# The first product of the second mixture as seven half-size products, its outputs whole in six banks

## The chip, the cores and the metric

One core of a Trainium2 chip runs the whole program. The metric is the device time of one execution in microseconds (us). "Measured" means the median of repeated executions; the profile is of a single execution, taken by the hardware profiler.

## The reference

Three parts follow each other. Attention with 32 packed queries gives `x` (2304 tokens of 512). A first mixture of four experts and a second one then follow, in float32:

```python
p = domain_probs / (domain_probs.sum(-1) + 1e-9)
for e in range(4):                                   # first mixture, w1[e] 512x1024, w2[e] 1024x512
    out += p[:, e:e+1] * (np.maximum(x @ w1[e], 0) @ w2[e])
h = out @ w_in                                       # second mixture, w_in 512x2048 (float64 in DRAM)
g = h - np.tanh(h)
result = g @ w_out                                   # w_out 2048x512 (float64 in DRAM)
```

## The kernel before, in words

Every product keeps float32 accuracy on TensorE by splitting both operands in a high and a low part: three matmuls (high by high, high by low, low by high) stand for one. TensorE's order of instructions is written out by hand, up to the end of the first mixture, as strings of letters (`START_A` to `LAST`), each of which calls one function. The other engines are ordered by a scheduler.

**First mixture** (to 690 us). Half of a half of the experts' features is worked on at a time, in two passes over the tokens. Its up products (`up_prod`, L469) are already made as seven half-size products (Strassen and Winograd's scheme), in matmuls of 288 columns; its down products (`down`, L527, matmul at L535) have 512 columns. Beside it `decode` (L331), called through `background` at each "_" of the strings, reads w_in and w_out as 64-bit words, rebuilds float32 from them with DVE, ACT and POOL, splits them, and stores high and low part in DRAM.

**Second mixture** (from 690 us). The 2304 tokens are 18 tiles of 128, taken in units of 4, 4, 4, 4 and 2; the 2048 features are halved (`cc`). An item is a unit, a half and two blocks of 128 features: 40 items. `s3` (L724) makes h of an item: per block 12 matmuls of 512 columns (the tokens; 256 in the last unit), K in four pieces of 128, three parts each. That is 640 + 320 matmuls at L734, 768 of them of 512 columns and 192 of 256. `elem` (L743) reads h straight from PSUM and makes g = h − tanh(h) of it (a polynomial where h is small, L751 to L760, up to 1024 wide); `elem_split` (L763) splits g in `gh` (ACT) and `gl` (DVE); `s4` (L777) multiplies by w_out into one PSUM tile per token tile, 864 matmuls of 512 columns at L790. The partial outputs of cc = 0 go through ACT (L803) to DRAM and are added on DVE (L807) at cc = 1. A half's weights lie in 16 SBUF tiles, loaded once. `x_T` (L557) transposes and splits a unit's tokens.

```python
for n in range(N + 2):
    s3(items[n]); x_T(...)        # TensorE: h of item n
    elem_split(items[n - 1]); elem(items[n])
    s4(items[n - 2])              # TensorE: outputs of the item before the last
```

PSUM has eight banks of [128, 512] float32; a tile [128, 2, 512] takes two of them.

## Time and profile before

| what | value |
|---|---|
| measured, median of 3 | 1092.18 us (1091.44 to 1094.64) |
| the profiled execution's own time | 1094.34 us |
| its span | 1092.6 us |
| TensorE's mean granted clock | 0.995 of full speed |
| first matmuls of the second mixture | 690.4 us |
| DMA in the whole program | 113.5 MB |

In the profile, a "group" is all instructions of one line, engine and tile; "<-" names the tile that an engine waited for, and who filled it. PE is TensorE, DVE the vector engine, ACT the scalar engine, POOL GpSimd, SP the engine that issues DMAs.

### The profile page before, as it was taken

How to read it: one execution, taken by the hardware profiler on the slowest of the kernel's cores; microseconds unless marked ns; L12 is line 12 of the kernel's file. 1: busy time of each engine (PE TensorE's matmuls, PEld its weight loads, DVE VectorE, ACT ScalarE, POOL GpSimd, SP SyncE). 2: the span in 40 equal slices, each digit the busy share in tenths (PEclk: the TensorE clock that was granted, in tenths of full speed). 3: DMA queues.
4: the chain of work that ended last, by engine and by line, in shares of the span. 5: the costliest groups of instructions: out<-in, count | busy, mean ns of one | idle time of the engine just before them, and what ended most of it. 6: DMA issues, size and time to landing. Idle time of an engine off the chain costs nothing.

```text
span 1092.6 us, 15816 instructions
## 1 busy us (share of the span) xinstructions
PE 1080.0 (99%) x6308; PEld 894.8 (82%) x6308; DVE 809.5 (74%) x1134; ACT 573.6 (53%) x853; POOL 215.3 (20%) x137
## 2 busy tenths in 40 slices
PE   8899999999999999999999999999999999999998
PEld 6677888888888878888888888888888888888887
DVE  4567888787787775888888786587676767777775
ACT  3345454544555355445545553466657556656464
POOL 0101223432542232334344332000000000000000
PEclk9899999999999999999999999999999999999999
DMA  9434124324333223332423321601001262202102
GB/s 342 174 93 174 59 78 145 128 75 154 125 107 135 78 77 97 116 136 84 151 94 121 130 96 64 283 1 39 5 35 39 78 231 97 77 1 77 64 14 77
DMA packets 38281, 113.51 MB, mean 104 GB/s; under 512 B 4288, under 2 KB 4288, under 8 KB 38208
## 3 DMA queue, kind: packets, MB, share of 16 engines
q1 hardware_dynamic: 38208, 112.51, 29.2%
q8 instruction: 49, 0.80, 0.3%
q14 instruction: 24, 0.20, 0.1%
HBM read 86.28 MB, written 26.21 MB: 103 GB/s over the span
## 4 chain that ended last, share of the span: by engine, by line
PE 85%; ACT 1%; DMA 0%; DVE 0%; issue 0%; DVEq 0%; SPq 0%
PE yps L535 32%; PE h3ps L734 18%; PE ops L790 18%; PE hpx L485 7%; PE hpz L485 6%; PE wps L390 2%; PE hps L437 1%; PE xps L570 1%; DMA wraw<-in_w_dram 0%; ACT wph L413 0%; PE qtp L314 0%; DVE p L496 0%; ACT w2h L143 0%; DVEq L873 0%; DVE f L350 0%
## 5 line engine op out<-in xcount | busy, mean ns | idle before, releaser
L734 PE MATMUL h3ps<-xh,ws 128*128 128x512 f32 (+1 forms) x640 | 186.7, 368 | 0.0
L790 PE MATMUL ops<-ws,gh 128*128 128x512 f32 x576 | 174.9, 391 | 0.0
L734 PEld LDWEIGHTS h3ps<-xh,ws 128*128 128x128 f32 x640 | 116.5, 188 | 20.2
L144 POOL TENSOR_TENSOR w2l<-wraw,w2h 128x1024 fp32r<-128x1024 f32 x32 | 82.4, 2576 | 246.2 <-ACT w2h L143 246.2
L546 DVE SCALAR_TENSOR_TENSOR x<-yps,pn,x 128x512 f32<-128x512 f32 x126 | 93.9, 745 | 43.3 <-PE yps L535 42.5
L790 PEld LDWEIGHTS ops<-ws,gh 128*128 128x128 f32 x576 | 107.2, 188 | 21.9 <-ACT gh L769 0.2
L535 PE MATMUL yps<-w2h,h0h 128*128 128x512 f32 x288 | 117.5, 408 | 1.9 <-DVE a2l L318 1.4
L734 PE MATMUL h3ps<-xl,ws 128*128 128x512 f32 (+1 forms) x320 | 117.7, 368 | 0.0
L535 PE MATMUL yps<-w2h,h0l 128*128 128x512 f32 x288 | 113.2, 393 | 0.0
L535 PE MATMUL yps<-w2l,h0h 128*128 128x512 f32 x288 | 112.8, 392 | 0.0
L535 PE MATMUL yps<-w2h,h1h 128*128 128x512 f32 x288 | 112.8, 391 | 0.0
L535 PE MATMUL yps<-w2h,h1l 128*128 128x512 f32 x288 | 112.4, 390 | 0.0
L535 PE MATMUL yps<-w2l,h1h 128*128 128x512 f32 x288 | 112.1, 389 | 0.0
L790 PE MATMUL ops<-ws,gl 128*128 128x512 f32 x288 | 108.7, 389 | 0.0
L769 ACT ACTIVATE gh<-g 128x512 fp32r<-128x512 f32 (+1 forms) x80 | 45.6, 583 | 84.3 <-DVE g L760 84.3
L535 PEld LDWEIGHTS yps<-w2h,h0h 128*128 128x128 f32 x288 | 54.1, 188 | 33.7 <-issue 21.0
L362 POOL TENSOR_TENSOR fo<-fo 128x512 f32<-128x512 f32 x32 | 43.3, 1352 | 193.6 <-DVE fo L358 105.7
L756 DVE SCALAR_TENSOR_TENSOR g<-z,h3ps 128x1024 f32<-128x1024 f32 (+1 forms) x40 | 44.5, 1113 | 43.0 <-ACT t L752 42.8
L770 DVE TENSOR_TENSOR gl<-g,gh 128x512 fp32r<-128x512 f32 (+1 forms) x80 | 49.8, 634 | 34.3 <-ACT gh L769 34.2
L751 ACT ACTIVATE z<-h3ps 128x1024 f32<-128x1024 f32 (+1 forms) x40 | 37.6, 941 | 68.5 <-PE h3ps L734 64.8
L734 PEld LDWEIGHTS h3ps<-xl,ws 128*128 128x128 f32 x320 | 60.3, 188 | 10.3
L535 PEld LDWEIGHTS yps<-w2h,h0l 128*128 128x128 f32 x288 | 54.0, 188 | 12.1
(156 smaller groups left out, 2402.0 us busy)
## 6 DMA issues: line engine op xcount, KB each, us to landing
wraw<-in_w_dram SPq DMA_DIRECT2D x64, 512.0 KB, 4.6
f<-in_win_dram SPq DMA_DIRECT2D x16, 512.0 KB, 4.6
win<-fo SPq DMA_DIRECT2D x16, 512.0 KB, 2.9
f<-in_wout_dram SPq DMA_DIRECT2D x16, 512.0 KB, 4.6
wout<-fo SPq DMA_DIRECT2D x16, 512.0 KB, 2.9
ws<-win SPq DMA_DIRECT2D x16, 512.0 KB, 5.3
ws<-wout SPq DMA_DIRECT2D x16, 512.0 KB, 5.3
kt<-in_kT_dram SPq DMA_DIRECT2D x16, 288.0 KB, 5.9
```

The source lines that it names most:

```text
L144: (eng or nc.vector).tensor_tensor(out=lo, in0=src, in1=f(hi), op=ALU.subtract)
L362: nc.gpsimd.tensor_tensor(out=lf, in0=lf, in1=sq, op=ALU.mult)
L390: nc.tensor.matmul(out=ps[32 * j:32 * j + 32, r, :], lhsT=ppbd[p][d, bi, j, 32 * r:32 * r + 32], rhs=raw[0, c, j // 2][d, j % 2, :],)
L485: nc.tensor.matmul(out=ps[:, ff, 0:HB], lhsT=W[a][:, slot, c0], rhs=x[b], start=(start and k == 0), stop=(stop and k == 2), skip_group_che ...
L535: nc.tensor.matmul(out=ps, lhsT=a[:, ff, o:o + 128], rhs=w[c, fp][:, ff], start=(k == 0), stop=(k == 11),)
L546: last[0] = nc.vector.scalar_tensor_tensor(out=x2[tt], in0=ps, scalar=pn[:, tt, e:e + 1], in1=x2[tt], op0=ALU.mult, op1=ALU.add,).ins
L734: nc.tensor.matmul(out=ps[:, ff, 0:n], lhsT=w[:, wl, kd, :], rhs=x[:, kd, :], start=(k == 0), stop=(k == 11),)
L751: nc.scalar.activation(out=z, in_=h, func=ACTF.Square)
L756: nc.vector.scalar_tensor_tensor(out=g, in0=z, scalar=C4, in1=h, op0=ALU.mult, op1=ALU.mult)
L769: nc.scalar.activation(out=hs[ff][:, 0:n], in_=g[:, ff], func=ACTF.Copy)
L770: nc.vector.tensor_tensor(out=ls[ff][:, 0:n], in0=g[:, ff], in1=f(hs[ff][:, 0:n]), op=ALU.subtract)
L790: nc.tensor.matmul(out=ops[u][t], lhsT=a[ff][:, d], rhs=w[:, wl], start=(i == 0 and ff == 0 and k == 0), stop=(i == 3 and ff == 1 and k == 2),
```

## The change

The 2304 tokens are now three units of 768 (u), the 2048 features eight groups of two blocks of 128 (NG); one of the 24 pairs is a chunk (N2), eight chunks to a unit. In a chunk the product [768 tokens x 512] by [512 x 256 features] is cut in two by two quarters (384 tokens, 256 of K, 128 features), and made as seven products of quarters or of sums of quarters: 6 matmuls of 384 columns each, 1008 in all.

- **Weights.** `decode` makes four sums per group on DVE, splits the seven slots, and stores them in `wing` (L371 to L393): seven stores per group where four were. It has 184 steps instead of 160; every fourth call of `background` takes a second step, and the strings have 60 "_" instead of 62.
- **Tokens.** `x_quad` (L613, transposes at L630) transposes a quarter of a unit (six transposes) into PSUM; DVE makes four sums per unit (L641, L646, L647, L652), `split` (L146 ACT, L147 DVE) splits seven quarters.
- **First product.** `s3` (L662, matmul at L681) makes the seven products of a chunk in two PSUM tiles, X and Z, of one bank each, in four steps; results in between are kept in SBUF by ACT (`keep`, L690) or added there by DVE (`add`, L694), with priority over the rest.
- **Elementwise.** `elem` works on two SBUF tiles [128, 768] per chunk, in place (L870 to L879; chunk 0 in pieces of 384). `elem_split` is L895 on ACT and L901 on DVE.
- **Second product.** `s4` (L908, matmul L918) sums all eight groups of a unit in PSUM, six token tiles in three PSUM tiles of two banks. At a unit's last chunk ACT copies each (L927), and it is stored (L928). Partial outputs are no longer stored and reloaded.
- **Loads.** `load_g` (L658) loads 1.835 MB per chunk into one of two buffers, `load_o` (L854) two tiles of 0.524 MB into two of four.
- **Order.** TensorE's order is written by hand to the end. Chunk 0's four steps and unit 0's quads stand in `LAST`; units 1 and 2 take their quads in `ops` tiles between the steps of chunk 1 and of chunks 9 and 10.

```diff
 LAST = (
-    "g7110 _ d710 _ g7111 _ d711 _ g7112 _ d712 _ g7113 _ d713 x00 d714 x01 d715 x10 d716 x11 d717 d718 "
+    "w0 g7110 _ d710 _ q00 g7111 _ d711 _ g7112 _ q01 d712 g7113 q02 d713 d714 q03 d715 s0 d716 s1 d717 s2 d718 s3 "
 )
...
+            s = k4t([128, 4, 256], F32R, "wins")
+            nc.vector.tensor_tensor(out=f(s[:, 0]), in0=a21, in1=a22, op=ALU.add)
+            nc.vector.tensor_tensor(out=f(s[:, 1]), in0=f(s[:, 0]), in1=a11, op=ALU.subtract)
             yield
+            nc.vector.tensor_tensor(out=f(s[:, 2]), in0=a11, in1=a21, op=ALU.subtract)
+            nc.vector.tensor_tensor(out=f(s[:, 3]), in0=a12, in1=f(s[:, 1]), op=ALU.subtract)
...
+        src = ps[:, :, 0:HT]
+        if q == 0:
+            x_tiles(u)
+            xr["T3"] = raw()
+            nc.scalar.activation(out=xr["T3"], in_=src, func=ACTF.Copy)
+            return
+        if q == 1:
+            xr["T1"] = raw()
+            nc.vector.tensor_tensor(out=xr["T1"], in0=xr["T3"], in1=src, op=ALU.subtract)
+            x_split(u, c, src)
+            x_split(u, "T1", xr["T1"])
...
+        else:
+            x_split(u, c, src)
+            nc.vector.tensor_tensor(out=xr["T1"], in0=src, in1=xr["T2"], op=ALU.subtract)
+            x_split(u, "T4", xr["T1"])
+            x_split(u, "T3", xr["T3"])
...
+    def load_g(n):
+        wg[n] = p_wp.tile([128, 2, 7, 256], F32R, tag="wp", name="wg")
+        nc.sync.dma_start(out=f(wg[n]).rearrange("p l s f -> p l (s f)"), in_=wing[n % NG])
...
+        def mul(ps, slot, c, start, stop):
+            k = 0
+            for kk in range(2):
+                for a, b in ((0, 0), (0, 1), (1, 0)):
+                    nc.tensor.matmul(
+                        out=ps, lhsT=wg[n][:, a, slot, 128 * kk:128 * kk + 128],
...
+        if step == 0:
+            mul(X, 0, "B11", True, False)
+            keep(c11, X)
+            mul(Z, 1, "B21", True, True)
+            add(c11, Z)
+        elif step == 1:
+            mul(X, 4, "T2", False, False)
+            keep(c12, X)
+            mul(Z, 3, "T1", True, False)
+            keep(c22, Z)
+        elif step == 2:
+            mul(X, 5, "T3", False, False)
+            add(c22, X)
+            mul(Z, 6, "B22", False, True)
+            add(c12, Z)
+        else:
+            mul(X, 2, "T4", False, True)
+            keep(c21, X)
...
+        def keep(t, ps):
+            with tc.high_priority(offset=PRIO):
+                nc.scalar.activation(out=t, in_=ps, func=ACTF.Copy)
+
+        def add(t, ps):
+            with tc.high_priority(offset=PRIO):
+                nc.vector.tensor_tensor(out=t, in0=ps, in1=t, op=ALU.add)
...
+        for k, hk in parts:
+            zk, tk, yk = (x if isinstance(k, slice) else x[:, k] for x in (z, t, y))
+            nc.scalar.activation(out=zk, in_=hk, func=ACTF.Square)
+            nc.scalar.activation(out=yk, in_=zk, func=ACTF.Square, bias=cst[:, 0:1])
+            nc.scalar.activation(out=yk, in_=yk, func=ACTF.Square, bias=cst[:, 1:2])
+            nc.scalar.activation(out=tk, in_=hk, func=ACTF.Tanh)
+            nc.vector.scalar_tensor_tensor(out=yk, in0=zk, scalar=R, in1=yk, op0=ALU.mult, op1=ALU.add)
+            nc.vector.tensor_tensor(out=tk, in0=hk, in1=tk, op=ALU.subtract)
+            nc.vector.scalar_tensor_tensor(out=hk, in0=zk, scalar=C4, in1=hk, op0=ALU.mult, op1=ALU.mult)
+            nc.scalar.activation(out=zk, in_=zk, func=ACTF.Relu, bias=cst[:, 2:3])
+            nc.vector.scalar_tensor_tensor(out=hk, in0=yk, scalar=S, in1=hk, op0=ALU.add, op1=ALU.mult)
+            nc.vector.copy_predicated(out=hk, mask=zk.bitcast(U32), data=tk)
...
+    def s4(n, ts, ff):
+        u, i = divmod(n, NG)
+        for t in ts:
+            if i == 0 and ff == 0 and t % 2 == 0:
+                ops[u, t // 2] = late["ops"].tile([128, 2, 512], F32, tag="ops", name="ops")
+            ps = ops[u, t // 2][:, t % 2]
+            c = 768 * ff + 128 * t
+            lo = gl[n][c // 512][:, c % 512:c % 512 + 128]
+            hi = gh[n][ff][:, 128 * t:128 * t + 128]
+            for k, (a, w) in enumerate(((hi, 0), (hi, 1), (lo, 0))):
+                nc.tensor.matmul(
+                    out=ps, lhsT=a, rhs=wo[n][ff][:, w],
+                    start=(i == 0 and ff == 0 and k == 0),
+                    stop=(i == NG - 1 and ff == 1 and k == 2), skip_group_check=True,
+                )
+            if i == NG - 1 and ff == 1:
+                r0 = 768 * u + 128 * t
+                o = u2t([128, 512], F32, "po")
+                with tc.high_priority(offset=PRIO):
+                    nc.scalar.activation(out=o, in_=ps, func=ACTF.Copy)
+                nc.sync.dma_start(out=out[r0:r0 + 128, :], in_=o)
...
+        order = [[("s", n, k)] if n < N2 else [] for k in range(4)]
+        m = n - 2
+        if m >= 0:
+            order[0].append(("o", m, range(0, 4), 0))
+            order[1] += [("o", m, range(4, 6), 0), ("o", m, range(0, 2), 1)]
+            order[2].append(("o", m, range(2, 4), 1))
+            order[3].append(("o", m, range(4, 6), 1))
+        if n == 1:
+            for k in range(4):
+                order[k].append(("q", 1, k))
+        if n == NG + 1:
+            order[2].append(("q", 2, 0))
+            order[3].append(("q", 2, 1))
+        if n == NG + 2:
+            order = [
+                [("s", n, 0), ("q", 2, 2)], [("s", n, 1), ("q", 2, 3)],
+                [("s", n, 2), ("o", m, range(0, 4), 0)], [("s", n, 3), ("o", m, range(4, 6), 0), ("o", m, range(6), 1)],
+            ]
...
```

DVE, one chunk in the steady part after the change (h3_7020 and h3_7021 are the chunk's two h tiles, h3_7152 is one of the next chunk's):

```order
L875 TENSOR_TENSOR t_7108<-h3_7020,t_7108 128x768 [waits DVE_49,Activation_49]
L876 SCALAR_TENSOR_TENSOR h3_7020<-z_7107,h3_7020 128x768 [waits DVE_49]
L875 TENSOR_TENSOR t_7128<-h3_7021,t_7128 128x768 [waits Activation_49]
L874 SCALAR_TENSOR_TENSOR y_7109<-z_7107,y_7109 128x768 [waits Activation_49]
L876 SCALAR_TENSOR_TENSOR h3_7021<-z_7127,h3_7021 128x768 [waits DVE_49]
L694 TENSOR_TENSOR h3_7152<-h3ps_7151,h3_7152 128x384 [waits PE_49,Activation_49]
L878 SCALAR_TENSOR_TENSOR h3_7020<-y_7109,h3_7020 128x768 [waits DVE_49]
L874 SCALAR_TENSOR_TENSOR y_7129<-z_7127,y_7129 128x768 [waits Activation_49]
L879 COPY_PREDICATED h3_7020<-z_7107,t_7108 128x768 [waits DVE_49]
L878 SCALAR_TENSOR_TENSOR h3_7021<-y_7129,h3_7021 128x768 [waits DVE_49]
L879 COPY_PREDICATED h3_7021<-z_7127,t_7128 128x768 [waits DVE_49,Activation_49]
L901 TENSOR_TENSOR gl_7120<-h3_7020,gh_7123 128x512 [waits Activation_49]
```

The next chunk's `add` stands inside this chunk's ten elementwise instructions. Before, five instructions of 1024 columns and two of `gl` made an item; now ten of 768, three adds and four of `gl` make a chunk.

TensorE at a unit's last chunk, before (ops_6723 to ops_6725 are the outputs of three token tiles):

```order
L790 MATMUL ops_6723<-ws_6585,gl_6851 128x512 [waits DVE_49]
L790 MATMUL ops_6724<-ws_6581,gh_6848 128x512 x2
L790 MATMUL ops_6724<-ws_6581,gl_6850 128x512
L790 MATMUL ops_6724<-ws_6585,gh_6849 128x512 x2
L790 MATMUL ops_6724<-ws_6585,gl_6851 128x512
L790 MATMUL ops_6725<-ws_6581,gh_6848 128x512 x2
```

and after (ops_6901 is the PSUM tile of two token tiles):

```order
L918 MATMUL ops_6901<-wo_7676,gh_7668 128x512 [waits DMAHW7_49]
L918 MATMUL ops_6901<-wo_7676,gh_7668 128x512
L918 MATMUL ops_6901<-wo_7676,gl_7649 128x512
L918 MATMUL ops_6901<-wo_7676,gh_7668 128x512 [waits Activation_49]
L918 MATMUL ops_6901<-wo_7676,gh_7668 128x512
L918 MATMUL ops_6901<-wo_7676,gl_7649 128x512
L681 MATMUL h3ps_7810<-xbh_6745,wg_7672 128x384
```

The second token tile of a pair now waits for ACT, which copies the first one out of the same PSUM tile; before, each had its own.

DVE where chunk 10's steps and unit 2's quads lie, after the change (h3_7812 and h3_7813 are the h tiles of chunk 9, h3_7988 of chunk 10; xps_7930 and xps_8004 are quads 1 and 2):

```order
L879 COPY_PREDICATED h3_7812<-z_7943,t_7944 128x768 [waits DVE_49,Activation_49]
L641 TENSOR_TENSOR xr_7937<-xr_7909,xps_7930 128x768 [waits PE_49]
L875 TENSOR_TENSOR t_7964<-h3_7813,t_7964 128x768 [waits Activation_49]
L876 SCALAR_TENSOR_TENSOR h3_7813<-z_7963,h3_7813 128x768 [waits DVE_49]
L646 TENSOR_TENSOR xr_8011<-xps_8004,xr_7937 128x768 [waits PE_49]
L647 TENSOR_TENSOR xr_7909<-xps_8004,xr_7909 128x768
L901 TENSOR_TENSOR gl_7956<-h3_7812,gh_7959 128x512 [waits Activation_49]
L901 TENSOR_TENSOR gl_7957<-h3_7812,gh_7959 128x256
L694 TENSOR_TENSOR h3_7988<-h3ps_7987,h3_7988 128x384 [waits Activation_49]
```

Chunk 10's first `add` (L694) now stands behind the quads' sums and chunk 9's elementwise instructions; before, a unit's tokens gave DVE two subtractions (L576).

## Rows read from the trace of the kernel before

**Rows 1.** Page, part 1: engine, busy us, share of the span, instructions.
```profile
PE 1080.0 (99%) x6308; PEld 894.8 (82%) x6308; DVE 809.5 (74%) x1134; ACT 573.6 (53%) x853; POOL 215.3 (20%) x137
```

**Rows 2.** Page, part 4: the chain that ended last, by line.
```profile
PE yps L535 32%; PE h3ps L734 18%; PE ops L790 18%; PE hpx L485 7%; PE hpz L485 6%; PE wps L390 2%; PE hps L437 1%; PE xps L570 1%; DMA wraw<-in_w_dram 0%; ACT wph L413 0%; PE qtp L314 0%; DVE p L496 0%; ACT w2h L143 0%; DVEq L873 0%; DVE f L350 0%
```

**Rows 3.** Windows: stretch, its us, busy us by engine, PEclk, DMA share, GB/s.
```profile
683.00:712.00 29.00, 29.00 (x133) 23.94 (x132) 16.32 (x17) 13.43 (x14) 0.00 (x0) 1.00 0.65 266
740.00:990.00 250.00, 250.00 (x1168) 209.19 (x1167) 179.56 (x186) 156.66 (x198) 0.00 (x0) 1.00 0.19 67
```

**Rows 4.** Chain in order of time: start us, us, matmuls of 512 columns.
```profile
734.15 5.44 PE h3ps L734 x24
```

**Rows 5.** Timeline, PE: start us, us, matmuls of 288 columns; eight transposes.
```profile
601.73 0.29 PE L485 MATMUL hpx<-a2h,wph 128*128 128x288 f32 x1
...
603.30 0.39 PE L535 MATMUL yps<-w2h,h0h 128*128 128x512 f32 x1
...
676.82 1.03 PE L570 MATMUL xps<-ident,x 128*128 128x128 f32 x8
```

**Rows 6.** Groups by shape, PE's weight loads, from 690 us.
```profile
L734 PEld LDWEIGHTS h3ps<-xh,ws 128*128 128x128 f32 x640 | 116.5, 188 | 20.2
```

**Rows 7.** Groups by shape, DVE, from 690 us: xcount | busy us, mean ns | idle before.
```profile
L760 DVE COPY_PREDICATED g<-mk,t 128x1024 f32<-128x1024 uint32 x32 | 44.4, 1389 | 1.1
L758 DVE SCALAR_TENSOR_TENSOR y<-z,y 128x1024 f32<-128x1024 f32 x32 | 39.1, 1223 | 21.1 <-ACT y L754 21.1
L770 DVE TENSOR_TENSOR gl<-g,gh 128x512 fp32r<-128x512 f32 x64 | 43.5, 687 | 27.7 <-ACT gh L769 27.5
L770 DVE TENSOR_TENSOR gl<-g,gh 128x256 fp32r<-128x256 f32 x16 | 6.3, 423 | 6.7 <-ACT gh L769 6.7
L760 DVE COPY_PREDICATED g<-mk,t 128x512 f32<-128x512 uint32 x8 | 6.1, 759 | 0.2
```

**Rows 8.** Groups by shape, DVE, before 690 us: a sum that reads PSUM, 256 wide.
```profile
L408 DVE TENSOR_TENSOR wsum<-wps,wsum 128x256 f32<-128x256 f32 x28 | 11.8, 422 | 10.7 <-ACT wph L407 8.6 <-issue 2.0
```

**Rows 9.** Timeline, DVE, 808 to 819 us: start us, us, instructions (x2: two of them).
```profile
808.36 1.29 DVE L770 TENSOR_TENSOR gl<-g,gh 128x512 fp32r<-128x512 f32 x2 [0.70 <-ACT gh L769]
...
817.51 1.38 DVE L760 COPY_PREDICATED g<-mk,t 128x1024 f32<-128x1024 uint32 x1
```

**Rows 10.** Groups by shape, ACT, from 690 us.
```profile
L769 ACT ACTIVATE gh<-g 128x512 fp32r<-128x512 f32 x64 | 39.4, 625 | 73.6 <-DVE g L760 73.6
L754 ACT ACTIVATE y<-y,cst 128x1024 f32<-128x1024 f32 x32 | 36.8, 1150 | 0.1
L803 ACT ACTIVATE po<-ops 128x512 f32<-128x512 f32 x18 | 9.7, 610 | 1.0 <-PE ops L790 1.0
```

**Rows 11.** Groups by shape, ACT, before 690 us.
```profile
L143 ACT ACTIVATE w2h<-wraw 128x1024 fp32r<-128x1024 f32 x32 | 33.5, 1047 | 0.7 <-DMA wraw<-in_w_dram 0.7
L407 ACT ACTIVATE wph<-wps 128x256 fp32r<-128x256 f32 x28 | 10.8, 386 | 27.9 <-DVE wpl L406 27.9
```

**Rows 12.** Timeline, ACT, same stretch: instructions that follow each other.
```profile
810.83 1.02 ACT L752 ACTIVATE t<-h3ps 128x1024 f32<-128x1024 f32 x1
811.73 1.16 ACT L753 ACTIVATE y<-z,cst 128x1024 f32<-128x1024 f32 x1
...
818.93 0.63 ACT L769 ACTIVATE gh<-g 128x512 fp32r<-128x512 f32 x1 [3.97 <-DVE g L760]
```

**Rows 13.** Page, part 6: DMA issues, KB each, median us to landing.
```profile
ws<-win SPq DMA_DIRECT2D x16, 512.0 KB, 5.3
```

**Rows 14.** Timeline, PE and then ACT, around a wait of PE.
```profile
140.34 0.40 PE L485 MATMUL hpx<-th,wph 128*128 128x288 f32 x1 [0.40 <-ACT p L492]
140.58 0.29 PE L485 MATMUL hpx<-tl,wph 128*128 128x288 f32 x1
...
139.66 0.63 ACT L492 ACTIVATE p<-hpx 128x576 f32<-128x576 f32 x1
```

More of the change, by code (lines that the diff above doesn't have):

```diff
@@ L134 @@
     cst = const.tile([128, 20], F32, name="cst")
-    win_s = [dram.tile([128, 2, 512], F32, name=f"win{m}") for m in range(16)]
+    wing = [dram.tile([128, 2, 1792], F32, name=f"wing{i}") for i in range(8)]
     wout_s = [dram.tile([128, 2, 512], F32, name=f"wout{m}") for m in range(16)]
-    part_s = [dram.tile([128, 512], F32, name=f"part{t}") for t in range(NT)]
     def f(ap):
@@ L549, in down @@
             ).ins
[L551 to L576 removed]
+    HT = 384
@@ L694 @@
             run(TURN)
-    pe_order.close()
-    pm.close()
-    psw.clear()
-    px[0] = ExitStack()
-    psx.append(pool("psx2", 2, px[0], space=PSUM))
-    ctx.push(px[0])
     for _ in bg:
         pass
+    pm.close()
+    pps.close()
     pa.close()
-    p_ws = pool("ws", 16)
-    p_xt = pool("xt", 1)
-    p_el = pool("el", 1)
-    wi, wo = {}, {}
-    order = [(cc, m) for cc in range(2) for m in range(8)]
-    loads = [(k, cc * 8 + m) for cc, m in order for k in (0, 1)]
-    nload = [0]
@@ L777, in s4 @@
[L777 to L789 removed]
+    late["el"] = pool("el", 2)
@@ new lines, with load_o @@
+    late["raw"] = pool("raw", 3)
+    late["hh"] = pool("hh", 4)
+    late["wo"] = pool("wo", 4)
+    late["gh"] = pool("gh", 4)
+    late["xb"] = pool("xb")
+    late["ops"] = pool("ops", 3, space=PSUM)
+    late["xz"] = pool("xz", 2, space=PSUM)
+    wo = {}
+    def load_o(n):
+        wo[n] = []
+        for b in range(2):
+            t = late["wo"].tile([128, 2, 512], F32R, tag="wo", name="wo")
+            nc.sync.dma_start(out=f(t), in_=wout_s[2 * (n % NG) + b])
+            wo[n].append(t)
@@ new lines, in elem @@
+    def elem(n, fb):
+        z, t, y = (late["el"].tile([128, 2, HT], F32, tag=k, name=k) for k in "zty")
+        h = hs[n][fb]
+        if n:
+            parts = [(slice(None), late_h[n][fb])]
+        else:
+            parts = [(k, h[k]) for k in range(2)]
+        for k, hk in parts:
[10 more added lines that the diff above has]
+            nc.vector.copy_predicated(out=hk, mask=zk.bitcast(U32), data=tk)
@@ new lines @@
+    load_g(1)
+    for fb in range(2):
+        elem(0, fb)
+    for n in range(1, N2 + 2):
+        if n + 1 < N2:
+            load_g(n + 1)
+        if n - 1 < N2:
+            load_o(n - 1)
+        order = [[("s", n, k)] if n < N2 else [] for k in range(4)]
[16 more added lines that the diff above has]
+            ]
+        for part in order:
+            for op in part:
+                {"s": s3, "o": s4, "q": x_quad}[op[0]](*op[1:])
+        if n == 1:
+            for fb in range(2):
+                elem_split(0, fb)
+        if n < N2:
+            for fb in range(2):
+                elem(n, fb)
+                elem_split(n, fb)
```

320 lines of the change are left out of this document (155 added, 165 removed).

## The prediction

> **What bounds the kernel now.** I read the page's first part first: TensorE is busy for 99% of the span, DVE for 74%, ACT for 53% [rows 1]. The chain of waits by line then says which of TensorE's work it is: the first product of the second mixture (L734) is 18% of the chain, the second one (L790) another 18% [rows 2]. The windows show the stage by itself: from 740 to 990 us TensorE is busy for 250.00 of 250 us at a clock of 1.00, while DVE has 179.56 us of work (72%) and ACT 156.66 (63%) [rows 3]. So here a matmul that goes is time that goes, for as long as DVE and ACT hand over in time; and DVE has only 28% to spare. That is the question of this change: it takes matmuls away, and gives DVE and ACT more instructions in a shorter stage.
>
> The profiled execution took 1094.34 us, 2.16 above the median of 1092.18. The sum below is made against the profiled one; 2.16 is taken off at its end. About 0.3% (3.3 us) is what a measurement of this kernel can tell from no change.
>
> **Matmuls.** The pace is taken from starts: 24 matmuls of 512 columns last 5.44 us, 0.2267 each [rows 4]; twelve of 288 start at 601.73 and the next line's first at 603.30, 0.1308 each [rows 5]. 384 columns lie between: 0.1308 + 96/224 x 0.0959 = 0.172 (in proportion to 512 it would be 0.170). 256 columns, by the same line, are 0.12. Removed: 768 x 0.2267 + 192 x 0.12 = 197.1 us, and 18% of the span in the chain is 196.7 [rows 2]. Added: 1008 x 0.172 = 173.4. **-23.7 us.** The bounds of this term: 0.170 gives -25.8; the weight load's 188 ns [rows 6] in its place gives -7.6. I take 0.172, since 0.1308 per matmul shows loads of 128 x 128 going by faster than 188 ns each. The 864 matmuls of the second product and the 72 transposes of the tokens stay.
>
> **A steady chunk.** TensorE: 42 x 0.172 + 36 x 0.2267 = 15.39 us. DVE: for 768 columns the middle of 1.223 and 0.687 is 0.954, copy_predicated 1.074 (1.389 and 0.759), a `gl` 0.687 or 0.423 [rows 7], an add of 384 from PSUM 0.55, between 0.422 [rows 8] and 0.687. Eight, two, two and two, and three of these are 13.65 us. An instruction that waits for nothing starts some 0.085 before its predecessor's end (two of 0.687 in 1.29 [rows 9]), so 17 of them need 12.3 net. ACT: 768 columns from SBUF are 0.84 plain (0.625 [rows 10] and 1.047 [rows 11]) and 0.94 with a bias (1.150 at 1024 [rows 10]); `keep` is 0.50 (0.386 [rows 11] to 0.61 [rows 10]). Ten elementwise, two `gh` and four `keep` are 12.7; ACT instructions overlap by 0.12 (810.83 + 1.02 - 811.73 [rows 12]), which leaves 11.0. Neither fills 15.39. But DVE also waits inside its own order: after a chunk's last add it needs the first tile's square and tanh from ACT (1.72 us with the hand-over), then the second tile's tanh (0.82), and 0.24 where an instruction reads the one just before it. The loop is 12.27 + 1.72 + 0.82 + 0.24 = 15.05 us, a margin of 0.35 us to TensorE's 15.39. So steady chunks stay bound by TensorE, and cost nothing beyond the matmuls; the margin is 0.02 us per DVE instruction.
>
> **Seams**, where TensorE waits:
> - Chunks 0 to 2. DVE has 36 instructions between chunk 0's third product and chunk 2's first, unit 1's quads among them: 20.5 us and 1.5 of waits for ACT, against 17.8 of TensorE's own: 4.2. The weights of chunk 2 can only start when chunk 0 leaves its buffer: 1.835 MB at the 266 GB/s shown [rows 3] are 6.9 us, and a load of 0.524 MB lands 5.3 us after its issue [rows 13], some 3.3 more than its transfer; 10.2 against chunk 1's 42 x 0.172 + 24 x 0.1 = 9.6 (eight transposes last 1.03 [rows 5]): 0.6 to 1.2. About 1.2 more where quads and the next outputs want the same banks. Together **+6.5**.
> - Chunk 10 takes two of unit 2's quads with nothing of the second product between its first two steps: only 0.6 us of transposes stand between product Z and the next use of X. DVE has 13 instructions in its way, 12.0 us with their waits, TensorE 8.7: **+3.3**.
> - Output pairs. Two token tiles share one PSUM tile, and the order shows the second's last three matmuls waiting for ACT, which copies the first. With ACT free this is 0.16 until the last matmul ends (0.40 less the 0.24 from start to start), 0.04 of hand-over (817.51 + 1.38 to 818.93 [rows 9, 12]), 0.61 for the copy [rows 10], 0.05 until TensorE starts (139.66 + 0.63 to 140.34) and 0.11 for a slow first matmul (0.24, not 0.13) [rows 14]: 0.97. ACT is in the middle of 768-column work inside the program, so a pair costs up to 0.84 more; I take 1.75 for the six pairs of units 0 and 1, 0.95 for the three at the end: **+13.3** (bounds 8.7 and 18). The Trainium skill (Perfetto Trace Analysis, "Matmuls") says that independent groups should rotate through different PSUM banks, so that the evacuation of one overlaps the next group. The halves of a pair lie in different banks, so by that rule these waits would not be, and the sum would be 13.3 lower; no row of the trace before shows a pair, and the order's wait decides for me.
> - The end. The last chunk's second product has 11.9 us of TensorE before it, and needs 13.1 of elementwise work: **+1.2**. Smaller waits, less a shorter tail: **+1.2**.
>
> **Costed at nothing.** The decode's 32 sums on DVE (32 x 0.42 = 13 us [rows 8]), its extra stores on SP and unit 0's quads lie in the first mixture, where TensorE's matmuls cover them: DVE is busy for 74% of the span [rows 1]. Uncovered they would cost up to 13. SP is also passed by chunk 0's weights, which queue behind the last stores; they are asked for some 15 us of matmuls ahead. Traffic: 24 x 1.835 + 48 x 0.524 = 69 MB in some 370 us are 187 GB/s, against 266 shown at a DMA share of 0.65 [rows 3].
>
> **Sum.** -23.7 + 6.5 + 3.3 + 13.3 + 1.2 + 1.2 = +1.8: 1096.1 for the profiled execution, **1094.0 us** for the median. The seams give back what the matmuls save.
>
> **Rivals.**
> - A, faster. The pairs don't wait, or the waits lie beside each other: for it speaks that ACT has 37% idle [rows 3], against it the wait in the order. Without the 13.3 the time is 1080.7; with half of all seams gone 1082. The rule on banks named above is this case.
> - B, slower: the elementwise loop becomes the period. It decides from 0.02 us more per DVE instruction on. For it: every duration for 768 columns is a middle, the margin is 0.35 us, and all 19 steady chunks pay at once; against it, 12.3 net is 80% of the chunk. At 0.03 to 0.05 more, the loop is 15.6 to 15.9 us, 19 x 0.2 to 0.5 = 4 to 10, and the seams, which DVE sets too, 3 to 5 more: 1101 to 1109, about 1105.
> - C, the reload of weights is slower than 187 GB/s. At 170 it is 407 us for the stage: over 1120. Against it: 266 shown [rows 3].
> - D, the change doesn't save what it says, since a matmul of 384 goes at the weight load's 188 ns [rows 6]: 16 us more, 1110. Against it: 0.1308 at 288 columns [rows 5].
> - E, every product waits for its evacuation, since X and Z are each one bank: five reuses x 0.95 x 24 = 114, about 1206. Against it: outputs of the chunk before the last stand between the steps. This is the other side of the same rule of the Trainium skill.
>
> **Chances.** Forecast 0.52: its own range is 1089 to 1100, of which faster 0.07, same 0.35, slower 0.10. A 0.18, faster. B 0.23, slower 0.20 and same 0.03. C, D and E together 0.07, slower. So faster 0.25, same 0.38, slower 0.37. The range reaches down to 1084, which leaves out half of A (0.09), and up to 1108, which leaves out the upper quarter of B (0.06) and C to E: 0.2 in all.
>
> **What would show it.** Right: matmuls of 384 columns at 0.172; a chunk near 15.4 us from first step to first step, with TensorE's idle time almost all in 20 or so places (chunks 1 and 2, chunk 10, the pairs, the end), some 25 us together; the pairs' idle time released by ACT's copies at L927. Wrong: TensorE waiting in every chunk for DVE's adds (B), no idle time at L918's pairs (A), waits on the weights' DMA (C), a pace of 0.19 (D).

## The result, and the profile after

The changed kernel takes 1109.14 us (median of 4, 1106.25 to 1112.71), the one before 1093.01 beside it (median of 4): a ratio of 1.0149, 95% interval 1.0114 to 1.0184. It is 16 us slower, 15 above the forecast and 1 above its range. The profiled execution took 1109.89 us, with a span of 1108.1.

The page's first part, after (busy us, share of the span, instructions; [rows 1] before):

```profile
PE 1070.8 (97%) x6356; PEld 904.1 (82%) x6356; DVE 881.1 (80%) x1313; ACT 637.3 (58%) x993; POOL 237.1 (21%) x145
```

TensorE has 9.2 us less work and 24.7 more idle time. The windows say where (us, busy us of PE, PEld, DVE, ACT and POOL, clock, DMA share, GB/s; [rows 3] before):

```profile
60.00:680.00 620.00, 610.58 (x3787) 502.89 (x3786) 509.37 (x769) 314.18 (x509) 229.83 (x134) 0.99 0.36 121
740.00:990.00 250.00, 239.09 (x1193) 212.84 (x1192) 201.48 (x270) 182.34 (x263) 0.00 (x0) 1.00 0.51 184
```

The second stretch is the second mixture; its 10.9 us of idle time are of the kind that was forecast. The first one is the first mixture, where TensorE was to lose nothing. Before, it was busy there for 617.48 us of the 620:

```profile
60.00:680.00 620.00, 617.48 (x3845) 510.85 (x3842) 484.93 (x747) 307.76 (x503) 208.05 (x126) 1.00 0.31 108
```

The same matmul in both kernels shows how much that is: the first of all matmuls of the down products, and the first of the last 108 of them (before, then after):

```profile
43.68 0.74 PE L535 MATMUL yps<-w2h,h0h 128*128 128x512 f32 x1
...
658.18 0.39 PE L535 MATMUL yps<-w2h,h0h 128*128 128x512 f32 x1
```

```profile
40.50 0.50 PE L570 MATMUL yps<-w2h,h0h 128*128 128x512 f32 x1
...
667.66 0.39 PE L570 MATMUL yps<-w2h,h0h 128*128 128x512 f32 x1
```

614.50 us became 627.16: **the first mixture lost 12.7 us** between these two ("the loss" below). Ahead of them the profiled run of before had a slow clock, so its own end of this stretch is 9.5 us earlier, not 12.7. From there to the end of the span it is 434.4 before and 440.4 after, +6.0, where the forecast had +1.8. So 9.5 of the 15.5 us between the two spans lie in the first mixture, and 6.0 behind it.

What TensorE waited for (us in total, times, longest), up to 690 us (without rows that before has too) and from there on:

```profile
PE hpx L520 <- ACT p L527: 4.8, 2, 4.4
PE yps L570 <- DVE x L581: 2.7, 5, 0.9
PE hpz L520 <- DVE p L531: 0.8, 2, 0.5
...
```

```profile
PE ops L918 <- ACT po L927: 10.4, 9, 1.8
PE ops L918 <- DVE xr L652: 4.3, 2, 3.8
PE h3ps L681 <- DVE h L694: 1.7, 1, 1.7
PE ops L918 <- DVE gl L901: 0.9, 1, 0.9
PE h3ps L681 <- ACT h L690: 0.3, 1, 0.3
```

The second table is the forecast's list of seams: nine pairs, chunks 0 to 2, chunk 10, the end. The first one is new. Its largest piece, in ACT's timeline, SP's and TensorE's (start us, us, idle before and releaser):

```profile
290.66 1.06 ACT L448 ACTIVATE wp<-wsum 128x1024 fp32r<-128x1024 f32 x1 [2.47 <-DVE wsum L447]
297.24 0.66 ACT L337 ACTIVATE fo<-f 128x512 f32<-128x512 uint32 x1 [5.51 <-DMA f<-in_wout_dram]
297.80 0.64 ACT L527 ACTIVATE p<-hpx 128x576 f32<-128x576 f32 x1
```

```profile
287.26 2.55 SPq L413 DMA_DIRECT2D wraw<-in_w_dram  x2
290.51 0.33 SPq L359 DMA_DIRECT2D f<-in_wout_dram  x1
```

```profile
298.49 0.61 PE L520 MATMUL hpx<-th,wp 128*128 128x288 f32 x1 [4.41 <-ACT p L527]
298.89 0.45 PE L520 MATMUL hpx<-tl,wp 128*128 128x288 f32 x1
```

The decode's word load goes out at 290.51 behind two weight loads, ACT stands at its first use (L337) for 5.51 us, the copy that frees TensorE's bank (L527) stands behind that, and TensorE then goes on at half clock: granted 0.50 from 298.5 to 302 us, a matmul busy for 0.45 us and more where 0.29 is usual.

### The profile page after: what moved, and what is told of

Its sections match the earlier page's. It is cut to its first block, busy times and chain, and to the rows that moved or that the text cites. A ratio compares the mean times of both kernels' runs of the same rounds, so it can differ in the third digit from the quotient of the medians.

```text
span 1108.1 us, 16290 instructions
## 1 busy us (share of the span) xinstructions
PE 1070.8 (97%) x6356; PEld 904.1 (82%) x6356; DVE 881.1 (80%) x1313; ACT 637.3 (58%) x993; POOL 237.1 (21%) x145
## 4 chain that ended last, share of the span: by engine, by line
PE 61%; DVE 13%; ACT 6%; DMA 3%; issue 2%; POOL 2%; SPq 0%; DVEq 0%; ACTq 0%; POOLq 0%
PE yps L570 19%; PE ops L918 16%; PE h3ps L681 14%; PE hpx L520 5%; PE hpz L520 4%; DMA f<-in_wout_dram 2%; PE wps L425 2%; DVE x L581 1%; DVE h0l L457 1%; PE hps L472 1%; DVE f L338 1%; DVE f L347 1%; DMA f<-in_win_dram 1%; ACT wp L448 1%; DVE p L531 1%
## 5 line engine op out<-in xcount | busy, mean ns | idle before, releaser
L918 PE MATMUL ops<-wo,gh 128*128 128x512 f32 x576 | 180.9, 395 | 14.7 <-ACT po L927 10.4
L918 PEld LDWEIGHTS ops<-wo,gh 128*128 128x128 f32 x576 | 106.5, 189 | 36.7 <-ACT po L927 14.3
L147 POOL TENSOR_TENSOR w2l<-wraw,w2h 128x1024 fp32r<-128x1024 f32 x32 | 83.5, 2610 | 216.6 <-ACT w2h L146 216.6
L918 PE MATMUL ops<-wo,gl 128*128 128x512 f32 x288 | 114.2, 396 | 0.9 <-DVE gl L901 0.9
L681 PE MATMUL h3ps<-xh,wg 128*128 128x384 f32 x384 | 107.2, 340 | 0.0
L520 PE MATMUL hpx<-th,wp 128*128 128x288 f32 x336 | 82.0, 299 | 4.9 <-ACT p L527 4.8
L870 ACT ACTIVATE z<-h 128x768 f32<-128x768 f32 (+1 forms) x50 | 40.7, 814 | 57.0 <-DVE h L694 57.0
L681 PEld LDWEIGHTS h3ps<-xh,wg 128*128 128x128 f32 x384 | 71.2, 190 | 2.0 <-ACT h L690 0.2
L520 PEld LDWEIGHTS hpx<-th,wp 128*128 128x128 f32 x336 | 59.2, 189 | 9.5 <-ACT p L527 5.7
L690 ACT ACTIVATE h<-h3ps 128x384 f32<-128x384 f32 x96 | 46.5, 484 | 35.0 <-PE h3ps L681 35.0
L681 PE MATMUL h3ps<-xbh,wg 128*128 128x384 f32 x224 | 63.0, 338 | 2.1 <-DVE h L694 1.7
L681 PE MATMUL h3ps<-xl,wg 128*128 128x384 f32 x192 | 65.0, 339 | 0.0
L918 PEld LDWEIGHTS ops<-wo,gl 128*128 128x128 f32 x288 | 54.3, 188 | 12.9 <-DVE gl L901 1.3
```

Of the source, the lines that this page charges most:

```text
L147: (eng or nc.vector).tensor_tensor(out=lo, in0=src, in1=f(hi), op=ALU.subtract)
L520: nc.tensor.matmul(out=ps[:, ff, 0:HB], lhsT=W[a][:, slot, c0], rhs=x[b], start=(start and k == 0), stop=(stop and k == 2), skip_group_che ...
L681: nc.tensor.matmul(out=ps, lhsT=wg[n][:, a, slot, 128 * kk:128 * kk + 128], rhs=x[c][b][kk] if isinstance(x[c][b], list) else x[c][b][:, k ...
L690: nc.scalar.activation(out=t, in_=ps, func=ACTF.Copy)
L870: nc.scalar.activation(out=zk, in_=hk, func=ACTF.Square)
L918: nc.tensor.matmul(out=ps, lhsT=a, rhs=wo[n][ff][:, w], start=(i == 0 and ff == 0 and k == 0), stop=(i == NG - 1 and ff == 1 and k == 2), ...
```

## Experiments

Of each, "loss" is the first mixture's between the two matmuls above, against the 614.50 us of before. It is read from one profile of each kernel: the six that have the changed kernel's first mixture as it is (the change itself, e3, e4, e6, e8, e14) lose 9.9 to 12.7, so two profiles less than 3 us apart tell little. Times are medians beside runs of the kernel before on the same chip.

**e1, no doubled steps.**

```diff
-            if calls[0] % 4 == 0:
-                next(bg, None)
```

> The changed kernel, but each call of the background takes one step of the decode, never two; what is left of the decode then runs as a lump behind the first mixture. In the profile after, down products of the first mixture come 9.5 us later than before at the end of the token passes (7.0 of it in one place, where ACT waits 5.51 us for a word load of the decode and TensorE 4.41 for the ACT instruction behind it, and then runs at half clock for 3.7 us). Theory 1: the doubled steps bring load, stores and use too close. Then the offset of the first mixture against before falls from 9.5 to under 4 us, and no wait of TensorE over 2 us is left there; the time gains up to 6 us, less what the lump costs behind the first mixture. Rival: the sums and stores themselves load DVE, SP and the DMA queues, in whatever order; then the offset stays at 6 us or more, in other places.

1135.89 us (ratio 1.0391, 1.0362 to 1.0421), and yet the loss was 2.8: these rows replace the first table of waits.

```profile
PE hpx L520 <- ACT p L527: 2.0, 2, 1.6
PE hpx L520 <- DVE p L531: 0.8, 1, 0.8
...
```

Theory 1's signs are there, but e1 takes off two things. `background` is called 156 times (158 before; "60" and "62" ahead of the prediction are not its calls), so e1 makes 156 of the 184 steps in this stretch, no more than the kernel before: neither doubled steps nor added ones. It shows that steps with the new sums and stores, in the place of old steps, cost at most 2.8. The lump behind cost far more than expected: TensorE waits for chunk 0's copies, 25.1 us in one piece.

```profile
PE h3ps L681 <- ACT h L690: 26.3, 3, 25.1
```

**e2, word loads earlier.** After a word tile's last use, the next load is issued at once:

```diff
-                st = load_words(wout[2 * i + b])
+                st = nxt[0]
                 yield
...
                 yield from words(st, lf)
+                if b == 0:
+                    nxt[0] = load_words(wout[2 * i + 1])
```

> The changed kernel, but each word load of the decode is issued one to three steps earlier, as soon as its predecessor's words are done; number and order of all other steps unchanged. Theory 1 (ACT stands in the first mixture behind word loads that were asked for too late, and TensorE behind ACT): the 5.51 us wait of ACT is gone, TensorE's 4.41 with it, the first mixture ends 6 to 8 us earlier, and the time falls from 1109 to 1101 to 1104. Rival (DVE's 32 extra sums are what makes the first mixture late, and the wait only shows it): the first mixture stays 6 us or more behind, the time above 1106.

1109.06 us (1.0136, 1.0105 to 1.0167), loss 10.7, and ACT waits at the same place for 4.86 us. The program asked earlier, but the load still went out at 291.61, right behind the same two weight loads on SP. The last thing that SP waited for ahead of it was the landing of a store, `wing<-win` (0.6 us in the changed kernel, 1.1 here): the load takes its buffer from the same pool as `win`, so asking earlier does not help before that store has landed. The edit didn't reach its aim, so it tells nothing of the theory.

**e5, doubled steps two calls earlier** (`calls[0] % 4 == 2`).

> The changed kernel, but the doubled step of the decode comes at the second, sixth, tenth call of the background instead of the fourth, eighth, twelfth: the same steps, two calls earlier. Without doubled steps the first mixture lost 2.8 us against before (from its first to its last but one common down product), with them 12.7, 7.0 of it where ACT waits 5.51 us for a word load; issuing loads earlier in the program left that place as it was, since the load went out at the same time, behind two weight loads on SP. Theory 1a: that place is an accident of what lies beside the load. Then with other steps in the place it goes, other waits come, and the first mixture loses 3 to 8 us: 1103 to 1107. Rival: the doubled steps cost what they cost wherever they stand (DVE, SP and buffers are full); then the loss stays at 11 to 14 us and the time at 1109.

1108.64 us (1.0127, 1.0109 to 1.0145). The 4.41 us wait is gone, the loss 9.1: other waits came, most of them for DVE. The time (0.5 us less) is the rival's. Three profiles with this phase (e5, e7, e9) lose 8.1 to 9.4, and e7 below is 3.0 us faster than e6, which differs in the phase alone: where the doubled steps stand matters for 0.5 to 3 us.

**e11, doubled steps alone, in the kernel before.** `background` of before with the two lines that e1 removed.

> The kernel before, with a second step of the decode at each fourth call: nothing of the change but this; the same work, closer together, and done with a fifth earlier. If the doubled steps by themselves cost what the first mixture lost (12.7 us as in the change, 9.1 with another phase), this kernel is 5 to 10 us slower than before, 1098 to 1104. If the loss needs the added sums, stores and tiles of the new decode too, it is within 3 us of before.

1105.58 us (1.0117, 1.0102 to 1.0131): **12 us slower than before from these two lines**, with a loss of 15.2 (its end of the stretch is 11.2 us later than in before, whose profile had its slow clock ahead of it). Its waits up to 690 us, and those of the kernel before:

```profile
PE yps L535 <- DVE x L546: 6.0, 8, 0.8
PE hpz L485 <- DVE p L496: 3.0, 9, 0.3
PE qtp L314 <- DVE wpl L398: 1.7, 1, 1.7
...
PE yps L535 <- ACT x L544: 1.1, 1, 1.1
...
```

```profile
PE hpz L485 <- DVE p L496: 1.0, 2, 0.7
...
PE yps L535 <- ACT x L544: 0.5, 1, 0.5
...
```

No long wait, but eighteen short ones for DVE. It has the same 1134 instructions as before, but is busy for 16 us more (page; [rows 1] before):

```profile
PE 1080.1 (98%) x6308; PEld 891.5 (81%) x6308; DVE 825.7 (75%) x1134; ACT 571.1 (52%) x853; POOL 216.1 (20%) x137
```

DVE's pieces are not larger: this decode repeats five steps, so with every fourth call doubled it is always the fourth and fifth that share a call, and these are work of POOL, ACT and SP. DVE's four decode instructions come every four calls instead of every five. What did grow stands ahead of one of the eight waits for `x` (DVE, POOL, TensorE):

```profile
286.24 2.67 DVE L422 SCALAR_TENSOR_TENSOR h0l<-u,h0h 128x576 fp32r<-128x576 f32 x1
285.89 2.40 POOL L144 TENSOR_TENSOR w2l<-wraw,w2h 128x1024 fp32r<-128x1024 f32 x1 [1.91 <-ACT w2h L143]
293.88 0.50 PE L535 MATMUL yps<-w2h,h0h 128*128 128x512 f32 x1 [0.76 <-DVE x L546]
```

Beside POOL the split took 2.67 us, where it takes 0.76 alone (at 302.80 in the kernel before), and the wait behind it is 0.76. Each of the eight waits for `x` comes 7.6 us after such a split of 2.65 to 2.67 us beside POOL; in the kernel before it takes 1.86 at most, and there is no wait for DVE's `x`. So the closer packing puts DVE's work beside POOL's. No run moves POOL's work away, so how much of the 12 us that makes is not shown.

**e12, the same steps singly, in 26 more calls.** e1, and one more "_" in EVEN, ODD, LASTA and LAST:

```diff
-    "g%(c)d%(p)d02 _ d%(l)d%(p)d7 g%(c)d%(p)d03 W%(e)d%(q)d0 _ d%(l)d%(p)d8 "
+    "g%(c)d%(p)d02 _ d%(l)d%(p)d7 _ g%(c)d%(p)d03 W%(e)d%(q)d0 _ d%(l)d%(p)d8 "
```

> The changed kernel with one step of the decode per call, never two, and 26 more calls spread over the strings of the first mixture (one more in EVEN, ODD, LASTA and LAST): 182 of the 184 steps lie there, singly. Theory: a doubled step puts some 2.7 us of DVE work and its ACT work in one place, where TensorE's buffers carry it over less, and this cost 12 us in the kernel before too; single steps with the same sums and stores cost what they did when they were never doubled, 2.8 us. Then the first mixture's loss falls from 12.7 to 3 to 6 us, and the time to 1100 to 1103. Rival: it is the density of steps, however they are spread, that fills DVE; then the loss stays at 8 us or more and the time above 1104.

1105.17 us (1.0115, 1.0101 to 1.0130), loss 7.3, between the two; by its time the rival holds. The five profiles with these strings (e12, e13, e15 to e17) lose 5.4 to 7.3. Single steps take back about half. The other half stays with 182 steps in this stretch where e1 and the kernel before have some 157: the added work is not free, however it is spread. Nor is the 2.7 us of DVE work in a doubled step the rule: by the order of the steps, 7 of some 36 doubled calls hold four of the decode's DVE instructions, the others two or none.

**e3, order at the units' ends.**

```diff
+            if m % NG == NG - 1:
+                order[1][-1] = ("o", m, (0, 2), 1)
+                order[2][-1] = ("o", m, (4, 1), 1)
+                order[3][-1] = ("o", m, (3, 5), 1)
```

> The changed kernel, but at a unit's last chunk the token tiles end in the order 0, 2, 4, 1, 3, 5, so that between the two tiles of a PSUM tile lie 6 matmuls of others. Same instructions. Theory: the second tile of a pair waits for ACT's copy of the first because both lie in one PSUM tile; in the profile after that is 10.4 us in 9 waits, and about 0.2 us more for each slow first matmul. Then under 2 us of these waits are left, and the time falls by 8 to 12, to 1097 to 1101. Rival: ACT's queue, not the shared tile, makes the wait (copies stand behind 768-column work); then more than 5 us stay, and the time falls by less than 5.

1099.62 us (1.0059, 1.0040 to 1.0079): 9.5 us less, and no wait of L918 for L927 is left. The shared PSUM tile made the waits; that ACT's queue did not is seen in e8, below, where ACT has less to do and they stay.

**e4, no reloads.** `load_g` and `load_o` return the tiles of chunk n − 2 from chunk 2 on.

> The changed kernel, but from chunk 2 on the weights of chunks 0 and 1 are used again, instead of loading those of the chunk: 22 of 24 loads of 1.835 MB and 44 of 48 of 0.524 MB are left out, so that the second mixture uses the wrong weights; instructions of TensorE, ACT and DVE are the same. In the profile after, a steady chunk lasts 15.64 us without any wait of TensorE: 42 matmuls of 384 at 0.1755 and 36 of 512 at 0.230, where 0.172 and 0.2267 were forecast. Theory: the traffic of the reloads (half of the DMA engines' time) slows TensorE's operands a little; then a chunk is near 15.4 us and the time 5 to 6 us lower. Rival: the pace belongs to these matmuls beside a busier DVE and ACT; then a chunk stays at 15.6.

1106.06 us (one run); a steady chunk still takes 15.64 us. The traffic of 69 MB costs the steady chunk nothing.

**e8, no polynomial** (lines L871, L872, L874, L876, L878 left out).

> The changed kernel without the polynomial of the elementwise stage: per h tile three of five DVE instructions (L874, L876, L878) and two of five ACT instructions (L871, L872) are left out, so that the output is wrong where h is small. TensorE's instructions are the same; DVE has 12.3 - 6 x 0.87 = 7 us per chunk instead of 12.3. Two questions. Pace: if the slower pace of a steady chunk (15.64 instead of 15.39) comes from DVE and ACT working beside TensorE, it falls to about 15.4; if it belongs to the sequence of matmuls, it stays at 15.64. Seams: if DVE's and ACT's work in line is what TensorE waits for at chunk 2 (3.8), chunk 10 (1.7), the pairs (10.4) and the end (0.9), the first two and the last go, and the pairs fall to the floor of nine waits of 0.69, 6.2; then the time falls by 12 to 15 us. If the transfers or the shared banks are what it waits for, they stay.

1105.65 us (one run, 3 us less, not 12 to 15), the chunk still 15.64, so the pace isn't DVE's and ACT's doing. The waits from 690 us on:

```profile
PE ops L913 <- ACT po L922: 10.6, 9, 2.6
PE ops L913 <- DVE xr L652: 2.9, 2, 2.6
```

Those for L694 and for the end are gone, as expected; the pairs stay at 10.6 (6.2 were expected), which fits e3; of the 3.8 us for L652 only 1.2 go.

**e14, products and outputs each in one piece** in 17 chunks (in the last but one, 30 output matmuls run twice, 6.8 us).

```diff
+            if m % NG in range(1, 7):
+                order = [p[:1] for p in order]
+                order[3] += [("o", m, range(6), 0), ("o", m, range(6), 1)]
```

> The changed kernel, but in 18 of the 24 chunks the four steps of a chunk stand together, and the 36 output matmuls of the chunk before the last behind them, in one piece. Two questions. Banks: X and Z are one bank each and each is used again in the next step; with the outputs between the steps a steady chunk had no wait of TensorE. If each product waits for its evacuation (the rule that independent groups should rotate through banks, case E of the forecast), a chunk gets 3 to 5 us longer, 55 to 90 us in all; if the other tile's six matmuls (1.05 us) cover an evacuation, less than 1 us a chunk. Pace: if the slower matmuls come from going to and fro between the products, the 36 in one piece run at 0.227 instead of 0.230.

1119.07 us (one run), chunks of 15.7 to 16.9. The start of a chunk's first product, then its second product's, one row at their start, one after 12 and one after 36:

```profile
924.73 0.33 PE L681 MATMUL h3ps<-xbh,wg 128*128 128x384 f32 x1
...
932.25 0.63 PE L918 MATMUL ops<-wo,gh 128*128 128x512 f32 x2
...
935.01 0.62 PE L918 MATMUL ops<-wo,gh 128*128 128x512 f32 x2
...
940.46 0.33 PE L681 MATMUL h3ps<-xbh,wg 128*128 128x384 f32 x1
```

The first 12 take 2.76 us, 0.230 each, the other 24 take 5.45, 0.227. So the second product's slower pace belongs here to the first dozen after a change of product, and the changed kernel changes eight times per chunk. It is no general rule: in the kernel before, twelve right after such a change took 2.72 (819.16 to 821.88), and the first product is no faster in one piece, 7.52 us for 42 or 0.179 each. Case E is out too: without outputs in between, products wait 4.1 us in all for L694, under half a microsecond per chunk. The Trainium skill (Perfetto Trace Analysis, "Matmuls") says that independent groups should rotate through different banks. Two are enough here: the other bank's six matmuls (1.05 us) cover an evacuation (0.48 on ACT, 0.55 on DVE).

**e6, e7, the seam at chunk 2, first try.** On e3, the matmuls of chunk 0's third output tile last (e6); the same with e5's phase (e7).

> The order of token tiles 0, 2, 4, 1, 3, 5 at the units' ends, as tried (it took 9.5 us off), and at chunk 2 all matmuls of chunk 0's third output tile at the end of the four steps instead of in the second: the same matmuls. In the profile after, TensorE waits 3.80 us there for DVE, which reads the last quad in that tile's banks, and then runs at half clock for about 6 us, some 3 us more. Theory: DVE is late by that much and no more, so 2 to 3 us of other matmuls in between hide most of the wait, and the clock doesn't fall: 4 to 7 us less, 1093 to 1096. Rival: DVE is the bound over chunks 1 and 2, and the wait only moves to the next product's add; then less than 2 us are gained, 1098 to 1100.

> All three: token tiles in the order 0, 2, 4, 1, 3, 5, chunk 0's third output tile last, and the doubled steps two calls earlier. If the three waits are independent, the gains add: 1109 less 9.5, less 4 to 7, less 3 to 6, so 1087 to 1093, at or below the kernel before. If the decode's doubled steps only move their wait, 1093 to 1096.

e6 took 1098.73 us (1.0043, 1.0027 to 1.0059), with the same wait of 3.8: I had moved the wrong tile. It is the second output tile that lies in the last quad's banks. e7 took 1095.73 (1.0019, 1.0009 to 1.0030), loss 8.1.

**e9, e10, work for POOL.** e3 and e5's phase, and `split(*xc[u][c], src, nc.gpsimd)` for the sums T1 to T4 of units 1 and 2 (e9); the decode's four sums on POOL too (e10).

> Token tiles in the order 0, 2, 4, 1, 3, 5, doubled steps two calls earlier, and for units 1 and 2 the low parts of the summed quarters (T1 to T4, of unit 2 T1 to T3) made by POOL instead of DVE: 7 of 22 splits and sums leave DVE's order, some 0.87 us each; POOL was idle there, and these operands are needed chunks later. The third output tile of chunk 0 stands where the change had it, since moving it left the 3.8 us wait as it was: it is the second output tile that waits. Theory: at chunks 1 and 2 DVE is busy without a gap, so 3 us fewer there cut the 3.8 us wait to under 2 and keep the clock up, and the wait of 1.7 at chunk 10 shrinks; 3 to 7 us less than the 1095.7 of the three edits together, 1089 to 1093. Rival: the quads' sums that read PSUM are in the way, not the splits, or POOL slows DVE down; then it stays at 1095 to 1097.

> The kernel of the run before it, and the decode's 32 sums of weights on POOL as well. Theory: DVE's 13 us of sums in the first mixture are part of the 8 us that it loses with the doubled steps moved; then it loses 4 to 6, and the time is 2 to 4 us below the other's. Rival: what the doubled steps cost there is their place among loads and waits, not DVE; then no difference of more than 1 us, or it is slower, since POOL takes longer for a sum and the decode's steps wait for it.

1098.36 (1.0047, 1.0033 to 1.0061) and 1102.37 (1.0081, 1.0066 to 1.0096): both worse than e7, which also has e6's move (0.9 us). In e9, while POOL works at unit 2's splits, some of DVE's instructions take twice their time (POOL, then DVE):

```profile
857.97 7.88 POOL L147 TENSOR_TENSOR xl<-xr,xh 128x768 fp32r<-128x768 f32 x3 [127.68 <-ACT xh L146]
```

```profile
857.78 0.94 DVE L147 TENSOR_TENSOR xl<-xps,xh 128x768 fp32r<-128x768 f32 x1
858.65 2.13 DVE L879 COPY_PREDICATED h<-z,t 128x768 f32<-128x768 uint32 x1
...
864.53 2.14 DVE L878 SCALAR_TENSOR_TENSOR h<-y,h 128x768 f32<-128x768 f32 x1
```

**e13, e15, e16, e17, towards a faster version.** e13 is e12 with e3. e15 and e16 add to it that the splits of T2, T3, T4 of units 1 and 2 come two to five chunks later, on POOL or on DVE. e17 is e13 with this order at chunk 2:

```diff
+                [("s", n, 0), ("o", m, range(2), 0), ("o", m, range(2), 1)], [("s", n, 1), ("o", m, range(2, 4), 0)],
+                [("s", n, 2), ("o", m, range(2, 4), 1), ("o", m, range(4, 6), 0)], [("s", n, 3), ("o", m, range(4, 6), 1)],
```

> The same with the token tiles in the order 0, 2, 4, 1, 3, 5 at the units' ends, which took 9.5 us off. If the two are independent: 1090 to 1094, about the kernel before or a little under it. If the density rival holds: 1095 to 1098.

> Single steps in more calls, token tiles 0, 2, 4, 1, 3, 5, and for units 1 and 2 the splits of three summed quarters (T2, T3, T4) two to five chunks later, one per chunk, their low parts on POOL. ACT and DVE have three instructions each less in both seams, 2.6 us of DVE; no sum waits for a tile that POOL reads. Theory (DVE's work in line is what TensorE waits for there): the 3.8 us wait falls to under 2, the clock stays up, chunk 2 lasts 17 to 19 us instead of 21 to 22.5, chunk 10 and 11 together 2 to 3 less: 1085 to 1090. Rival: the wait belongs to the reads of the last quad's bank, which stand behind other things; then less than 1 us is gained: 1092 to 1094.

> The same, with the late splits on DVE. A steady chunk has 15.64 - 15.05 = 0.6 us of margin in DVE's loop and gets 0.87 more in six chunks: up to 0.3 each, 2 us in all, if the loop is as tight as the forecast had it (rival B's mechanism), nothing if it has more room. So 0 to 2 us above the run before it.

> Single steps in more calls, token tiles 0, 2, 4, 1, 3, 5, and at chunk 2 the matmuls of chunk 0's first output tile (both blocks) ahead of those of the second, which now begin behind the second step. TensorE has some 2.4 us more to do before it touches the last quad's banks. Theory (the wait is that bank): the 3.8 us fall to 1 to 2, the clock falls less, the time by 2 to 4 from 1093.1, so 1089 to 1091, faster than before. Rival (DVE is the bound there): product Z of the second step waits for the add that stands behind the same L652, for about 2 us, in its place; then the gain is 1 to 2, 1091 to 1092, the same as before.

e13: 1093.13 us (1.0011, 0.9999 to 1.0022), loss 5.4. e15: 1097.45 (1.0050, 1.0037 to 1.0064). e16: 1093.31 (1.0005, 0.9996 to 1.0015): on DVE the six late splits cost nothing, and their chunks still take 15.64 us, so its loop has at least 0.87 us to spare in a chunk; with POOL in DVE's place the program is 4 us slower. Neither touched the 3.8 us wait, since L652 stands ahead of these splits in DVE's order. e17: **1091.63 us (0.9997, 0.9985 to 1.0008)**, 17.5 below the change and level with before. Its seam:

```profile
719.39 0.44 PE L681 MATMUL h3ps<-xh,wg 128*128 128x384 f32 x1 [1.58 <-DVE h L694]
```

The wait has shrunk from 3.80 to 1.58 and the clock stays at 1.00 there, but it now waits for the add behind L652, as the rival had it. No version beat the kernel before beyond the noise.

## Why the prediction was wrong

**The step that failed** is "costed at nothing": the decode's work in the first mixture "lie[s] in the first mixture, where TensorE's matmuls cover" it, argued from DVE's 74% over the span. I had counted what was added (32 sums, 13 us of DVE, bound 0 to 13) and not that every fourth call now makes two steps. In its place the runs show a loss of 12.7 us. It is 2.8 with neither added nor doubled steps (e1) and 5.4 to 7.3 with the added steps made singly (e12 and after it), so about half of it is the added work, half the doubling; and the doubling alone costs the old kernel 12 us (e11). The loss is within the 13 of the bound, though not for the bound's reason: DVE's busy share says how much work fits, not when it comes nor what it runs beside. It is no fixed amount of work either: with the same 1313 instructions DVE is busy for 867.2 us in e1, 875.7 in e12 and 881.1 here, in the order of the losses, and four of this kernel's five waits for `x` come within 5 us of a DVE instruction that took 2.6 to 3.0 us beside POOL (0.4 to 0.8 alone). That fits e10, which is e9 with the sums moved from DVE to POOL and 4.0 us slower; but that POOL is the cause here is argued from the rows, not tested. None of the five rivals was this.

**Matmuls**, −23.7: direction right, pace a little off. Two rows of the steady part, 15.64 us apart, start the same matmul of two chunks; L681 then starts after 12 matmuls, and L918 after 12 of those:

```profile
893.38 0.63 PE L918 MATMUL ops<-wo,gh 128*128 128x512 f32 x2
...
909.02 0.63 PE L918 MATMUL ops<-wo,gh 128*128 128x512 f32 x2
...
911.78 0.33 PE L681 MATMUL h3ps<-xbh,wg 128*128 128x384 f32 x1
...
913.89 0.63 PE L918 MATMUL ops<-wo,gh 128*128 128x512 f32 x2
```

0.230 and 0.176 instead of 0.2267 and 0.172: 0.25 us per chunk, 6.0 in 24. With the second product's pace in it, this term is −17.7. The row that I took for 512 columns [rows 4] was a run of 24; those for 288 [rows 5] were twelve after a change, but 384 lies above the line between the two.

**The steady chunk** is bound by TensorE, as forecast: no wait in it, and the durations were right.

```profile
L879 DVE COPY_PREDICATED h<-z,t 128x768 f32<-128x768 uint32 x30 | 32.2, 1074 | 1.9 <-ACT z L877 0.8
L874 DVE SCALAR_TENSOR_TENSOR y<-z,y 128x768 f32<-128x768 f32 x31 | 29.4, 952 | 0.5 <-ACT y L872 0.4
L694 DVE TENSOR_TENSOR h<-h3ps,h 128x384 f32<-128x384 f32 x45 | 24.9, 554 | 12.3 <-PE h3ps L681 12.3
```

1.074, 0.952 and 0.554 against 1.074, 0.954 and 0.55. Rival B is out; its margin of 0.35 us was too small (e16).

**The seams**, +25.5: the waits behind 690 us sum to 17.6. Pairs 10.4 (13.3), chunks 0 to 2 and quads 4.3 (6.5), chunk 10 1.7 and 0.3 (3.3), the end 0.9 (1.2). To the waits comes the clock, which the forecast left out:

```profile
720.00:725.00 5.00, 1.20 (x6) 0.85 0.56 237
725.00:730.00 5.00, 5.00 (x14) 0.50 0.01 3
730.00:735.00 5.00, 5.00 (x25) 0.96 0.30 78
```

After 3.80 us without work it is at 0.50 of 2.4 GHz, the lower level: from 724.77 to 730.88 us 18 matmuls take 6.11 us, and 3.5 elsewhere, so 2.6 us are lost. With that the seams come to about 20. Each of the 14 waits also costs some 0.27 us beside its idle time (an estimate from the one of 1.78: 842.21, 844.38 and 844.95 are starts 2.17 and 0.57 apart, where 0.23 and 0.46 are usual), which makes about 24 of the 25.5. Rival A (pairs don't wait, by the rule on banks) is out: their halves lie in two banks, and waited 10.4 us, because they share a tile that the program tracks as one (e3, e8). Sum behind the first mixture: −17.7 and 24 are about +6; measured +6.0. That this sum was +1.8 in the forecast comes from the pace; the seams' total was right although single seams were 2 to 3 us off and the clock was missing, which is luck in part.

What stays open: how much of the first mixture's loss is DVE's slowing beside POOL and how much the density and pairing of the steps, and what makes the first dozen matmuls of the second product slower.

## What to carry to other kernels

Background work beside a bound engine costs by when it comes and what it runs beside, not only by its sum: before a change packs the same steps closer, look at how long the bound engine's buffers carry it over and which engines then run at once, and test the packing alone. When two outputs share a tile, end them apart, not one after the other. A saving in matmuls is only had where no seam opens; here 18 us saved met over 20 of seams, and even with the pairs' waits and the doubled steps mended the kernel stood level.
